# A gated convolution and MLP in one program: the last column of one MLP block computed with the others, and the last output pair loaded inside the loop

## The chip, the cores and the metric

The program runs on one core of a Trainium2 chip. A core has a matrix engine (TensorE, PE in the profile; the loading of its weights is shown as PEld), a vector engine (VectorE, DVE), an activation engine (ScalarE, ACT), a general engine (GpSimd, POOL) and a synchronising engine (SyncE, SP). Each works through its own list of instructions in order and waits on semaphores for the others. SP, ACT and POOL also issue DMA transfers between the large memory (HBM) and the on-chip memory (SBUF); sixteen DMA engines carry them out. Matrix products land in PSUM, eight banks of 128 partitions by 512 floats.

The metric is the time of one execution on the device in microseconds (us); lower is better. The time before is the median of three executions.

## The reference

```
g = sigmoid((x * gate_w).sum(-1))                  # x = A_u, 2048 tokens x 512
a = irfft(rfft(u) * rfft(K)) + u * Dskip           # long convolution; K from A, B, C, dt
b = gelu(B_x @ w1 + b1) @ w2 + b2                  # 512 -> 1792 -> 512
out = g * a + (1 - g) * b
```

All is in float32. The arithmetic of b is called the MLP here and that of a the convolution. The kernel computes b from A_u as its input (the reference passes x = A_u to both).

## The kernel before, in words

The kernel has two parts, one after the other. `front` makes the MLP, the first stage of the convolution's transform of the signal, and the filter's taps (`tk_d`, in HBM). `conv` does the rest of the convolution and the final mix.

**The front.** All of it is written as tasks of a planner (`Plan`). A task has an engine, an estimated duration, the data that it reads and writes, and a due time. `Plan.run` plays the tasks through: whichever engine can start first takes, among its tasks that are ready, the one with the smallest due. The order found in this way is the order in which the instructions are written out; the due times stand in a long string, `DUES`, one number for each task in the order in which the tasks are made. So a task whose due is larger than that of all others is written when its engine has no other task ready.

The MLP takes the 2048 tokens as 8 blocks of 256 and goes over them twice, each time with half of the 14 columns of 128 hidden units: blocks b = 0 to 15 (`NB` = 16), and in each block four steps j = 0 to 3 of 2, 2, 2 and 1 columns. `hidden` makes the hidden values of a step (L985 to L987 on PE, gelu and a rounding on ACT at L1002 and L1005, the low part on DVE at L1012). `output` multiplies them with w2: for each half s of the block's tokens three products for each column (L1028, L1029, L1031) into one of two PSUM accumulators, `acc0` and `acc1`. After a block's last step ACT multiplies the accumulator by 1 - g into a tile `io` (L1053); in the second pass POOL then adds `io` onto the output in HBM with an accumulating DMA (L1066).

Not all of the second pass is done in the front. Of block 15 all w2 products, and of block 14 the last column (j = 3), are put in a list, `late`, which `conv` works off. In block 14 the accumulators are thus closed after j = 2 and go out without their last column.

**The joint.** `conv` has tile pools of its own in the memory that the front's pools leave. In the program of before its first PSUM tiles lie on the front's banks: the signal tiles `p2u` of step 0 on those of `acc0` and `acc1`, those of step 1 on two of the banks of `ph`. The first product tiles `v` of step 0 lie on the bytes of the two `io` tiles. An engine that writes such a tile first waits until the old one has been read.

**The loop of `conv`.** Sixteen steps s. In each, PE makes the second stage of the transform of the signal (`signal`, `p2u`) and of the taps (`taps`, `p2k`, both L1218), DVE multiplies the two (`product`, L1240 to L1245), PE transforms back (`inverse`, `pa`, L1257), ACT copies the result to `sa` (L1269), and SP stores it to `t4_d` in HBM (`turn`, L1271). Beside this POOL loads, in step 6 to 12, one pair of output rows each from HBM (`mix(0)` to `mix(6)`, L1296): the MLP's share to which the convolution's share is to be added. The loads of the last stage's inputs (`quarter`, L1263) are issued by POOL and SP as the groups of eight results are complete, and for the last group by ACT inside `turn(15)`. There `mix(7)`, the load of the last output pair, stands as the last but one of ACT's issues.

**The rest and the last stage.** `rest` works off `late`: three columns before the last `inverse` (`N_REST` = 3), the other thirteen behind the loop, each column three products (L1308 to L1310). The sums of block 14's column (two tiles, `odd`) are multiplied by 1 - g on ACT (L1361) and added on DVE to output pair 6 (L1384); those of block 15 are multiplied and added to output pair 7 in one DVE instruction each (L1379). Then for each of eight pairs of output rows m, PE makes the last product (`pb`, L1373, six PSUM tiles in turn), DVE multiplies it by g and adds it to the loaded pair (L1386), and SP stores the pair (L1392, 512 KB; the last pair in three pieces by SP and ACT, L1390). The two instructions of L1379 stand in DVE's list just before the first of pair 5 and of pair 6.

Of the kernel before, what the change touches and what calls it, by code (L numbers as in the profile page):

```python
# [71 lines left out]
D_SD = -116.26  # L72
D_B2 = 90.72
N_LATE = 2
N_REST = 3
N_LANES = 8
SWITCH = 0.1
# [64 lines left out]
"""  # L142

GROUP = 8
# [205 lines left out]
def gated_mix(  # L350
# [52 lines left out]
    def front(pool, psum, keep, attic, loft, den, pr):  # L403
# [612 lines left out]
        def output(i, t):  # L1016
            b, j = divmod(i, 4)
            fs = cols(i)
            hi, lo, hk, lk = halves(i)

            def products(s, a):
                ss = slice(s * P, (s + 1) * P)
                seeded = b < NSB
                start = j == 0 and not seeded
                for n, f in enumerate(fs):
                    w = f % FH
                    h, l = hi[:, n, ss], lo[:, n, ss]
                    nc.tensor.matmul(a, h, wh[1][w], start=start, stop=False, skip_group_check=seeded)  # L1028
                    nc.tensor.matmul(a, h, wl[1][w], start=False, stop=False, skip_group_check=seeded)  # L1029
                    stop = (j == 2 and n == 1) if b == NB - 2 else j == 3  # L1030
                    nc.tensor.matmul(a, l, wh[1][w], start=False, stop=stop, skip_group_check=seeded)  # L1031
                    start = False

            ws = [(n, f % FH, 1) for f in fs for n in ("wh", "wl")]
            for s in range(2):
                if b == NB - 1 and s >= 2 - N_LATE:
                    for n, f in enumerate(fs):
                        late.append((s, hi[:, n], lo[:, n], wh[1][f % FH], wl[1][f % FH]))
                    continue
                q = (2 * b + s) % N_ACC  # L1040
                n = 3 * len(fs)
                if b == NB - 2 and j == 3:
                    late.append((2 + s, hi[:, 0], lo[:, 0], wh[1][fs[0] % FH], wl[1][fs[0] % FH]))
                else:
                    mm(
                        0.2305 * n, lambda s=s, q=q: products(s, acc[q]), t + LAG + D_OUT * (j == 3),
                        [hk, lk, *ws], [("acc", q)],
                    )
                if j == 3:
                    n = b % NSB * 2 + s  # L1050
                    r = (2 * b + s) % 2
                    act(
                        0.58, lambda n=n, q=q, r=r: nc.scalar.mul(io[r], acc[q], gate[:, 1, n : n + 1]),  # L1053
                        t + D_EV, [("acc", q), ("gate", b % NSB)], [("io", r)],
                    )
                    if b + 1 < NSB:
                        seed(q, t + D_EV)
                    if b < NSB:
                        move(
                            256, lambda n=n, r=r: nc.sync.dma_start(out[n], io[r]), t,  # L1060
                            [("io", r)], [("v", n)],
                        )
                    else:
                        move(
                            512,
                            lambda n=n, r=r: nc.gpsimd.dma_start(out[n], io[r], accum_op=ALU.add),  # L1066
                            t, [("io", r)], [("v", n)], queue="GP",
                        )
# [109 lines left out]
    def conv(pool, ps, late, attic, loft, den, pr):  # L1178
# [86 lines left out]
        def turn(s):  # L1265

            for n in (2 * s, 2 * s + 1):
                sa = sas[n % 6]
                nc.scalar.copy(sa, pas.pop(n))  # L1269
                g, k = divmod(n, GROUP)  # L1270
                nc.sync.dma_start(t4_d[g, :, k].rearrange("e c q d -> (c q) e d"), sa)  # L1271
                if k < GROUP - 1:
                    continue
                if g == 3:
                    for h in (8, 16):
                        quarter(nc.sync, 2, h)
                    for h, n in ((0, 4), (4, 4), (8, 8), (16, 8)):
                        quarter(nc.scalar, g, h, n)
                    quarter(nc.scalar, 2, 24)
                    mix(7, nc.scalar)  # L1280
                    quarter(nc.scalar, g, 24)
                elif g < 2:
                    for h in (0, 8, 24) if g else (0, 8):
                        quarter(nc.gpsimd, g, h)
# [3 lines left out]
        def mix(k, on):  # L1288

            r = 5 + 2 * k if k < 7 else 0  # L1290
            if r < N_ATTIC:
                mos[k] = attic[:, r : r + 2]
            else:
                r -= N_ATTIC
                mos[k] = loft[:, r * D : (r + 2) * D].rearrange("p (s d) -> p s d", s=2)
            on.dma_start(mos[k], out[2 * k : 2 * k + 2].rearrange("s p d -> p s d"))  # L1296
# [32 lines left out]
        for s in range(16):  # L1329

            if s % 2 or s == 0:
                if s < 10:
                    factors((s + 5) // 2)
            for n in range(16 + 4 * s, 20 + 4 * s) if s < 4 else ():
                fetch(n)
            for n in range(2 * s + N_ROOM, min(2 * s + N_ROOM + 2, 32)) if s > 3 else ():
                nc.sync.dma_start(us[n], tu_d[ko[n]])
            product(s)
            if 1 < s + 1 < 16:
                signal(s + 1)  # L1340
            if s + 2 < 16:
                if s and s % 2 == 0:
                    matrices(s // 2 + 1)
                taps(s + 2)
            if s == 15:
                rest(N_REST)
            inverse(s)
            if s == 6:
                quarter(nc.gpsimd, 0, 24)
            if s == 10:  # L1350
                for g in range(2):
                    quarter(nc.gpsimd, g, 16)
            if 6 <= s < 13:
                mix(s - 6, nc.gpsimd)
            if s == 12:
                quarter(nc.gpsimd, 2, 0)
            turn(s)
        rest(16)
        odd = [pool.tile([P, D], F32, tag=f"v{r}", name=f"odd{r}", bufs=2) for r in range(2)]
        for r in range(2):  # L1360
            nc.scalar.mul(odd[r], accs[2 + r], gate[:, 1, 12 + r : 13 + r])  # L1361

        for m in range(8):
            tag = "pa" if m % 3 == 2 else f"pu{m % 3}"
            for i in range(2):
                pb = ps.tile([P, D], F32, tag=f"{tag}{i}", name=f"pb{m}{i}", bufs=1)
                t = 2 * m + i
                parts = [slice(0, D // 2), slice(D // 2, D)] if t == 15 else [slice(0, D)]
                for cs in parts:
                    for b in range(2):  # L1370
                        j = 2 * t + b
                        row = t3[:, j - 8] if j > 7 else den[:, j]
                        nc.tensor.matmul(  # L1373
                            pb[64 * b : 64 * b + 64, cs], g1t[:, min(j, 1)], row[:, cs], start=True, stop=True
                        )
                z = mos[m][:, i]
                if i == 0 and 5 <= m < 5 + N_LATE:
                    r = m - 5
                    nc.vector.scalar_tensor_tensor(  # L1379
                        mos[7][:, r], accs[r], gate[:, 1, 14 + r : 15 + r], mos[7][:, r], ALU.mult, ALU.add  # L1380
                    )
                if m == 1 and i == 0:
                    for r in range(2):
                        nc.vector.tensor_add(mos[6][:, r], mos[6][:, r], odd[r])  # L1384
                for h, cs in enumerate(parts):
                    nc.vector.scalar_tensor_tensor(  # L1386
                        z[:, cs], pb[:, cs], gate[:, 0, t : t + 1], z[:, cs], ALU.mult, ALU.add
                    )
                    if m == 7:
                        (nc.sync, nc.scalar, nc.sync)[i + h].dma_start(out[t][:, cs], z[:, cs])  # L1390
            if m < 7:
                nc.sync.dma_start(out[2 * m : 2 * m + 2].rearrange("s p d -> p s d"), mos[m])  # L1392
# [81 lines left out]
```

## Time and profile before

| what | value |
|---|---|
| time, median of 3 | 506.92 us (506.61 to 507.43) |
| time of the profiled execution | 507.3 us |
| its span, first to last instruction | 505.5 us |
| mean clock granted to TensorE | 0.996 |
| bytes moved by DMA | 107.56 MB |
| output pair loads (L1296) issued by POOL, by ACT | 7, 1 |

The profile shows one execution. Its own time is 1.8 us above its span and 0.4 us above the median. Times within it are counted from its first instruction. A row of the timeline gives start, duration, engine, source line, operation and tiles, and in brackets how long the engine was idle before it and who released it. A "q" behind an engine's name marks an entry of its instruction queue, for instance the issue of a DMA.

### The profile page before, as it was taken

The page shows a single profiled execution, that of the slowest core. Times are in us where ns is not written, and L with a number is a line of the kernel's source. Part 1 is how long each engine was busy: PE and PEld are TensorE (multiplying, and loading weights), DVE is VectorE, ACT ScalarE, POOL GpSimd, SP SyncE. Part 2 cuts the span into 40 slices and gives each one's busy share as a digit, 9 for nine tenths or more (in the row PEclk, how much of TensorE's full clock was granted, in tenths as well). Part 3 has the DMA queues.
Part 4 walks back from the last instruction along what each step waited for, and adds up shares of the span by engine and source line. Part 5 has one row for each costly group of instructions (what it writes and reads, how often), then busy time and mean ns, then how long its engine had stood idle before and what let it go on. Part 6 is the DMA issues. An engine that isn't in the chain of part 4 may idle for free.

```text
span 505.5 us, 12181 instructions
## 1 busy us (share of the span) xinstructions
PE 495.2 (98%) x4802; PEld 379.0 (75%) x4802; DVE 429.2 (85%) x817; ACT 365.0 (72%) x632; POOL 38.3 (8%) x78
## 2 busy tenths in 40 slices
PE   8999999999999999999999999999999999999994
PEld 7898888898989889888988888998989522222551
DVE  4977999999999999999999999999940197877455
ACT  6999997899997789997767998636834465565310
POOL 2000000000000000001010020110100100231000
PEclk9999999999999999999999999999999999999998
DMA  8978686531858622855987244950477999989897
GB/s 286 350 280 278 188 243 213 161 126 43 280 138 246 200 73 72 254 168 116 232 217 241 75 64 128 186 100 3 154 219 169 259 389 389 338 305 391 294 344 299
DMA packets 81569, 107.56 MB, mean 213 GB/s; under 512 B 39284, under 2 KB 43784, under 8 KB 80968
## 3 DMA queue, kind: packets, MB, share of 16 engines
q1 hardware_dynamic: 74792, 82.80, 51.8%
q0 software_dynamic: 6016, 20.70, 15.4%
q10 hardware_dynamic: 704, 3.28, 1.8%
q8 instruction: 38, 0.62, 0.5%
q14 instruction: 19, 0.16, 0.1%
HBM read 61.14 MB, written 45.62 MB: 211 GB/s over the span
## 4 chain that ended last, share of the span: by engine, by line
PE 93%; DMA 2%; SPq 1%; DVE 1%; issue 1%; ACT 0%; POOL 0%; DVEq 0%; POOLq 0%
PE pk L788 12%; PE ph L985 10%; PE acc L1028 10%; PE ph L987 10%; PE ph L986 10%; PE acc L1029 9%; PE acc L1031 9%; PE p2k L1218 5%; PE p2u L1218 5%; PE pa L1257 3%; PE ph L489 3%; PE pb L1373 2%; DMA tk<-tk_d 1%; SPq L830 1%; DMA tk_d<-sk 1%; PE acc L1101 1%
## 5 line engine op out<-in xcount | busy, mean ns | idle before, releaser
L985 PE MATMUL ph<-xh,wh 128*128 128x256 f32 x448 | 127.5, 285 | 0.0
L987 PE MATMUL ph<-xh,wl 128*128 128x256 f32 x448 | 126.8, 283 | 0.0
L986 PE MATMUL ph<-xlo,wh 128*128 128x256 f32 x448 | 126.7, 283 | 0.0
L985 PEld LDWEIGHTS ph<-xh,wh 128*128 128x128 f32 x448 | 85.2, 190 | 6.9 <-issue 4.0
L986 PEld LDWEIGHTS ph<-xlo,wh 128*128 128x128 f32 x448 | 85.1, 190 | 2.1
L987 PEld LDWEIGHTS ph<-xh,wl 128*128 128x128 f32 x448 | 85.2, 190 | 0.0
L1028 PE MATMUL acc<-wh,hh 128*128 128x512 f32 x208 | 84.3, 405 | 0.0
L1029 PE MATMUL acc<-wl,hh 128*128 128x512 f32 x208 | 81.7, 393 | 0.0
L1031 PE MATMUL acc<-wh,hl 128*128 128x512 f32 x208 | 81.4, 391 | 0.0
L1002 ACT ACTIVATE ph<-ph,b1t 128x256 f32<-128x256 f32 x112 | 50.5, 451 | 25.0 <-PE ph L987 23.2
L788 PE MATMUL pk<-y,den 128*32 128x64 f32 x2048 | 61.4, 290 | 0.0
L788 PEld LDWEIGHTS pk<-y,den 128*32 128x32 f32 x2048 | 57.2, 136 | 2.6 <-issue 0.7
L1012 DVE TENSOR_TENSOR hl<-ph,hh 128x512 fp32r<-128x512 f32 (+1 forms) x62 | 38.2, 618 | 18.3 <-ACT hh L1005 10.8
L1028 PEld LDWEIGHTS acc<-wh,hh 128*128 128x128 f32 x208 | 39.1, 188 | 19.4 <-issue 8.8
L750 DVE TENSOR_TENSOR y<-y,ea 128x64 f32<-128x64 f32 (+4 forms) x80 | 45.3, 566 | 0.8 <-POOL y L740 0.3
L1031 PEld LDWEIGHTS acc<-wh,hl 128*128 128x128 f32 x208 | 39.1, 188 | 8.8
L1029 PEld LDWEIGHTS acc<-wl,hh 128*128 128x128 f32 x208 | 39.1, 188 | 6.1
L1226 ACT COPY k<-p2k 128x512 f32<-128x512 f32 x32 | 18.6, 586 | 27.2 <-issue 11.3
L594 DVE TENSOR_TENSOR loft<-den,zz 128x256 f32<-128x256 f32 (+2 forms) x48 | 37.2, 774 | 0.2
L595 DVE TENSOR_TENSOR loft<-den,zz 128x256 f32<-128x256 f32 (+2 forms) x48 | 37.2, 775 | 0.1
L763 DVE TENSOR_TENSOR y<-y,loft 128x2048 f32<-128x2048 f32 x16 | 36.6, 2286 | 0.4 <-ACT loft L713 0.2
L1005 ACT CAST hh<-ph 128x512 fp32r<-128x512 f32 (+1 forms) x62 | 33.0, 533 | 4.3 <-PE acc L1029 2.4
(197 smaller groups left out, 873.3 us busy)
## 6 DMA issues: line engine op xcount, KB each, us to landing
tk_d<-sk SPq DMA_DIRECT2D x32, 256.0 KB, 5.3
t_d<-sa SPq DMA_DIRECT2D x32, 256.0 KB, 5.1
tu_d<-attic SPq DMA_DIRECT2D x40, 128.0 KB, 3.5
attic<-in_xt_dram SPq DMA_DIRECT2D x16, 256.0 KB, 4.3
attic<-in_xs_dram SPq DMA_DIRECT2D x16, 256.0 KB, 5.0
xl_d<-xlo SPq DMA_DIRECT2D x8, 512.0 KB, 5.9
xh_d<-xh SPq DMA_DIRECT2D x8, 512.0 KB, 3.9
out_dram<-io SPq DMA_DIRECT2D x16, 256.0 KB, 3.1
```

What stands on the lines that cost most here:

```text
L594: vec(2 * m, lambda: vv.tensor_mul(t, a, br), due, [ka, *kb], [kt])
L750: nc.vector.tensor_mul(both(n, 64 - 3 * n, n), both(0, 64 - n, n), an)
L788: nc.tensor.matmul(pks[q][32 * j : 32 * j + 32, :, gg], x[:, r, :, ch], y[:, r, :, ch], start=(r == 0), stop=(r == 1), skip_group_check=True,)
L985: nc.tensor.matmul(p, h, xh[xk][:, d], start=(d == 0), stop=False)
L986: nc.tensor.matmul(p, h, xlo[xk][:, d], start=False, stop=False)
L987: nc.tensor.matmul(p, lo, xh[xk][:, d], start=False, stop=(d == 3))
L1002: nc.scalar.activation(phs[q][:, n], phs[q][:, n], AF.Gelu_apprx_tanh, bias=b1t[:, f : f + 1])
L1012: nc.vector.tensor_sub(lo, phs[q][:, 0:nf], hi.bitcast(F32))
L1028: nc.tensor.matmul(a, h, wh[1][w], start=start, stop=False, skip_group_check=seeded)
L1029: nc.tensor.matmul(a, h, wl[1][w], start=False, stop=False, skip_group_check=seeded)
L1031: nc.tensor.matmul(a, l, wh[1][w], start=False, stop=stop, skip_group_check=seeded)
L1218: nc.tensor.matmul(out[64 * i : 64 * i + 64], w, x, start=True, stop=True)
```

## The change

There are three edits that belong together.

1. Block 14's last column is no longer put off. `ODD = ()` names the halves whose column would be; being empty, it makes `output` add six products (three for each half of the tokens) as two tasks of the front, and move the accumulators' closing to them. Both tasks get the due 10000, which is larger than every other. The multiplication at L1053 and the accumulating DMA at L1066 of block 14 now come behind these tasks. In `conv` the six products of `rest`, the two ACT multiplications (L1361) and the two DVE additions (L1384) fall away.
2. `mix(7)` moves from ACT's issues in `turn(15)` to POOL's in step 13 of the loop. In POOL's list it then stands behind `quarter(2, 0)` of step 12.
3. The two DVE instructions that add block 15's sums to output pair 7 move from their places before pairs 5 and 6 to a place before the whole last stage.

```diff
+ODD = ()
...
-1773 415 2550 11 2497 14 320 242 499 507 544 671 244 133 477 228 163 91 19 193 589 536 459 592 210 132 229
...
+1773 415 10000 2550 11 10000 2497 14 320 242 499 507 544 671 244 133 477 228 163 91 19 193 589 536 459 592
...
-                    stop = (j == 2 and n == 1) if b == NB - 2 else j == 3
+                    stop = (j == 2 and n == 1) if b == NB - 2 and s in ODD else j == 3
...
-                if b == NB - 2 and j == 3:
+                if b == NB - 2 and j == 3 and s in ODD:
                     late.append((2 + s, hi[:, 0], lo[:, 0], wh[1][fs[0] % FH], wl[1][fs[0] % FH]))
...
                     quarter(nc.scalar, 2, 24)
-                    mix(7, nc.scalar)
                     quarter(nc.scalar, g, 24)
...
-            if 6 <= s < 13:
+            if 6 <= s < 14:
                 mix(s - 6, nc.gpsimd)
             if s == 12:
                 quarter(nc.gpsimd, 2, 0)
...
-        odd = [pool.tile([P, D], F32, tag=f"v{r}", name=f"odd{r}", bufs=2) for r in range(2)]
-        for r in range(2):
+        odd = {r: pool.tile([P, D], F32, tag=f"v{r}", name=f"odd{r}", bufs=2) for r in ODD}
+        for r in ODD:
             nc.scalar.mul(odd[r], accs[2 + r], gate[:, 1, 12 + r : 13 + r])

+        for r in range(N_LATE):
+            nc.vector.scalar_tensor_tensor(
+                mos[7][:, r], accs[r], gate[:, 1, 14 + r : 15 + r], mos[7][:, r], ALU.mult, ALU.add
+            )
...
-                if i == 0 and 5 <= m < 5 + N_LATE:
-                    r = m - 5
-                    nc.vector.scalar_tensor_tensor(
-                        mos[7][:, r], accs[r], gate[:, 1, 14 + r : 15 + r], mos[7][:, r], ALU.mult, ALU.add
-                    )
                 if m == 1 and i == 0:
-                    for r in range(2):
+                    for r in ODD:
                         nc.vector.tensor_add(mos[6][:, r], mos[6][:, r], odd[r])
```

6 rows, old and new, of the table DUES are left out of this document.

## The prediction

> **What bounds the kernel now.** I read the page first, then the chain of work that ended last, then the timelines of the two places that the change touches, then the transfers there. First the shares of the chain by engine, and two pieces of the chain in order of time (start, us, what):
>
> ```profile
> PE 93%; DMA 2%; SPq 1%; DVE 1%; issue 1%; ACT 0%; POOL 0%; DVEq 0%; POOLq 0%
> ...
> 396.56 5.76 DMA tk<-tk_d
> ...
> 402.36 2.49 PE p2k L1218 x8
> ```
>
> PE carries 93% of the chain. It leaves PE at two places. At the joint between front and conv it runs over the store and the reload of the taps: the first tap tile is issued at 396.56, lands at 402.32, and PE starts on it at 402.36. The other place is the end, behind PE's last products. So work moved from the tail into the front is paid in full on PE unless the joint has room, and what it saves is only what the tail's own limit gives back.
>
> The tail, by the stretch (PE, PEld, DVE, ACT, POOL busy, clock, DMA share, GB/s):
>
> ```profile
> 473.00:478.00 5.00, 5.00 (x26) 3.22 (x25) 1.60 (x3) 1.93 (x4) 0.00 (x0) 1.00 0.64 232
> 478.00:483.00 5.00, 5.00 (x24) 4.14 (x23) 0.00 (x0) 0.00 (x0) 0.00 (x0) 1.00 0.98 333
> 483.00:494.00 11.00, 11.00 (x52) 4.42 (x52) 7.59 (x12) 1.26 (x2) 0.00 (x0) 1.00 0.98 354
> 494.00:501.00 7.00, 4.93 (x28) 1.72 (x24) 5.97 (x10) 0.00 (x0) 0.00 (x0) 1.00 1.02 391
> ```
>
> From 478 to 501 the DMA engines are full (0.98 to 1.02). Between 473 and 478 they are not (0.64, so 1.8 us of 5 idle). DVE looks as full behind 486, and the chain of waits ends in DVE; it does not show a queue in which a transfer stands after its issue. These rows do: SP's first stores, the landing of the first of them (issued at 487.74), that of the last pair's pieces, and the two queues (packets, MB, share) in 483 to 490, then SP's in 494 to 500.
>
> ```profile
> 487.74 4.63 SPq L1392 DMA_DIRECT2D out_dram<-attic  x3
> ...
> DMA to landing us min/median/max: 7.8/7.8/7.8
> ...
> DMA to landing us min/median/max: 4.5/4.6/4.6
> ...
> q10 hardware_dynamic: 435, 2.46, 97.5%
> q1 hardware_dynamic: 3, 0.00, 0.0%
> ...
> q1 hardware_dynamic: 1207, 2.32, 100.9%
> ```
>
> The store of 487.74 (SP's q1) moved nothing before 490: ACT's loads (q10) held the engines. Stores then drain at 2.32 MB in 6 us at full share, 0.387 MB/us, or 1.36 us for a pair of 512 KB (0.524 MB). Eight pairs need 10.8 us, and the last pieces still take 4.5 us, where a 256 KB store with free engines takes 2.4 (quoted below). So I read the tail as **bound by bytes**: it ends when the loads are in and eight pairs have drained, not when DVE is done.
>
> **The change, part by part.**
>
> *Six products into the front.* The timelines of PE, its weight loads and ACT at the joint:
>
> ```profile
> 391.96 0.39 PE L1028 MATMUL acc<-wh,hh 128*128 128x512 f32 x1
> ...
> 394.71 0.28 PE L985 MATMUL ph<-xh,wh 128*128 128x256 f32 x1
> ...
> 397.46 0.28 PE L987 MATMUL ph<-xh,wl 128*128 128x256 f32 x1
> 397.67 3.65 PE L1218 MATMUL p2u<-den,pr 128*64 128x512 f32 x16
> ...
> 399.16 0.43 PEld L1218 LDWEIGHTS p2u<-den,pr 128*64 128x64 f32 x4 [0.43 <-DVE hl L1012]
> ...
> 402.91 0.19 PEld L1218 LDWEIGHTS p2k<-tk,pr 128*64 128x64 f32 x3 [0.36 <-DMA tk<-tk_d]
> ...
> 394.91 0.69 ACT L1053 ACTIVATE io<-acc,gate 128x512 f32<-128x512 f32 x1 [0.60 <-PE acc L1031]
> ...
> 398.27 0.37 ACT L1005 CAST hh<-ph 128x256 fp32r<-128x256 f32 x1
> ```
>
> Twelve such products ran from 391.96 to 394.71, 0.229 each; six cost 1.37. A due above all others puts them where PE has nothing else ready, and PE has no gap there: behind the last hidden product (397.46 + 0.12 = 397.58), ending at 398.95. The three of the first half end at 397.58 + 0.69 + 0.16 (a product's 0.39 outlasts its 0.23 pace) = 398.43. ACT is busy until 398.27 + 0.37 = 398.64, and its two multiplications of 0.69 now come behind that, to 399.35 and 399.95. Step 0's signal tiles lie on the banks that they read, so this is a new wait: PE stands before `p2u` until 399.4, with everything behind it in its list, instead of starting at 397.67. The second tile is free in time. The old wait of 0.43 at 399.16 for DVE is over by then. Sixteen products at 0.215 end at 399.4 + 3.44 = 402.84, against 402.36, when the first tap tile was used. But the second tap tile held PE until 402.91 in any case, and the first sum needs both. So 1.73 us of delay meets as much slack: between -0.07 (both tiles needed; PE itself is busy until 402.84, so earlier tap tiles bring no more) and 0.48 (the first half counts); I take **0.05**, by the second row. Without this cover it would cost 1.73. What is late next is the DMA again, not PE.
>
> *The accumulating DMAs of block 14.* POOL's second issue, the landing of all fourteen of L1066, and what DVE and PE do next:
>
> ```profile
> 395.89 0.86 POOL L1066 DMA_DIRECT2D out_dram<-io  x1 [0.43 <-ACT io L1053]
> ...
> DMA to landing us min/median/max: 4.0/5.0/7.6
> ...
> 404.64 0.69 DVE L1240 TENSOR_TENSOR v<-p2u,k 128x512 f32<-128x512 f32 x1 [5.54 <-ACT k L1226]
> 405.50 0.69 DVE L1241 TENSOR_TENSOR v<-p2u,k 128x512 f32<-128x512 f32 x1 [0.17 <-ACT k L1226]
> ...
> 407.90 0.68 DVE L1245 TENSOR_TENSOR v<-v,z 128x512 f32<-128x512 f32 x1
> ...
> 408.85 0.21 PEld L1257 LDWEIGHTS pa<-v,pr 64*64 64x64 f32 x8 [0.81 <-DVE v L1245]
> ```
>
> They follow ACT by 0.3 (395.60 to 395.89), so at 399.65 and, POOL needing 0.86 for each, 400.5. With the fourteen issues' landing of 4.0 to 7.6, median 5.0, `io` is free at 404.65 and 405.5, just when DVE first writes `v` there (404.64, 405.50). A late landing holds all six DVE products behind it; PE waits for them only beyond 0.27 (408.58 to 408.85). Bounds 0 and 408.1 - 405.5 - 0.27 = 2.3; I take **0.1**, near the median. Nothing else stands behind them in POOL's queue until the loop's sixth step.
>
> *The load of pair 7.* Its issue on ACT, POOL's last entry, SP's last stores of `t_d`, the landing of the last two of these, and ACT's first load:
>
> ```profile
> 484.13 0.79 ACTq L1296 DMA_DIRECT2D attic<-out_dram  x1
> ...
> 471.36 0.55 POOL L1263 DMA_DIRECT2D den<-t_d  x1 [7.89 <-DMA t_d<-sa]
> ...
> 471.07 6.79 SPq L1271 DMA_DIRECT2D t_d<-sa  x5
> ...
> DMA to landing us min/median/max: 2.4/2.4/2.4
> ...
> 479.96 1.15 ACTq L1263 DMA_DIRECT2D den<-t_d  x2
> ```
>
> Its 0.524 MB leave the full stretch: 1.36 at the drain's pace, 1.48 at the 354 GB/s of its own stretch; I take **-1.45**. Only one of ACT's issues, the last `quarter`, was behind it. On POOL it stands behind the `quarter` of 471.36, thus at 471.9, and nothing after it. Its bytes then run in 473 to 478, where 1.8 us is free, but beside the last five stores of `t_d` (from 471.07), the last two of which now land in 2.4 us and release ACT's loads at 479.96. What doesn't fit pushes these: 0 if the gaps take all, 1.36 if the stores wait for the whole of it. I take **+0.25**, near the low end since the gaps are wider than the load.
>
> *The end of DVE's list.* PE's first products of the last stage, the landing of ACT's first loads, four rows of DVE, and the landing of all pair loads (L1296):
>
> ```profile
> 484.97 3.65 PE L1373 MATMUL pb<-den,g1t 128*64 128x512 f32 x16
> ...
> DMA to landing us min/median/max: 4.6/4.6/4.6
> ...
> 487.62 1.28 DVE L1384 TENSOR_TENSOR loft<-loft,odd 128x512 f32<-128x512 f32 x2
> 488.83 2.72 DVE L1386 SCALAR_TENSOR_TENSOR attic<-pb,gate,attic 128x512 f32<-128x512 f32 x4
> ...
> 494.49 0.74 DVE L1379 SCALAR_TENSOR_TENSOR attic<-acc,gate,attic 128x512 f32<-128x512 f32 x1
> 495.15 1.40 DVE L1386 SCALAR_TENSOR_TENSOR loft<-pb,gate,loft 128x512 f32<-128x512 f32 x2
> ...
> DMA to landing us min/median/max: 7.1/8.9/12.6
> ```
>
> PE's `rest` ends 1.37 sooner, at 483.6, but the last group's first rows, issued at 479.96, land after 4.6: the last stage can start at 484.6, 0.4 sooner than 484.97. DVE loses two additions (487.62 to 488.83, 1.21) and has the two instructions of L1379 (494.49 to 495.15, 0.66 each) done before the first product; their wait for pair 7 (471.9 + 12.6 = 484.5 at the longest) holds nobody. That is 2.53 + 0.4 sooner for the stores. The two ACT multiplications that fall away were on no path. As the stores queue at the engines, I count **0**; it would be 2.9 if that queue were not there.
>
> Sum: 0.05 + 0.1 - 1.45 + 0.25 = **-1.05**, all in the profiled execution: 507.3 becomes 506.25. That execution is 0.4 above the median, which I carry: 506.92 - 1.05 = **505.9 us**.
>
> **The rivals.**
>
> *DVE ends the tail.* For it: the chain ends in DVE, and DVE is full from 486. Against it: the stores' 7.8 and 4.5 us. Then -2.9 + 0.15 = 504.2.
>
> *The moved load meets the last stores.* For it: in the loop, with the engines full, `t_d` stores take far longer than 2.4 (landing of all of L1271 from 440 on):
>
> ```profile
> DMA to landing us min/median/max: 2.4/5.3/10.9
> ```
>
> If the two queues share evenly, the last two stores' 0.524 MB take twice 1.36: +1.36 in place of +0.25, 507.0, no change. The Trainium skill (DMA: Bandwidth & Descriptors, "Queues, rings and completion order") says that each engine goes round the queues with work, packet by packet, which speaks for this; the trace's q1, empty beside a full q10 at 487.74 to 490, disagrees. If the last store takes the loop's median of 5.3, the loads start 2.9 late: -1.45 + 2.9 + 0.15 = +1.6, **508.5, slower**. It decides at 1.3 us: beyond it the change loses.
>
> *The joint pays.* An `io` landing of 6.2 to 7.6, or the full 0.48 before the taps, gives +0.5 to +2.3: 506.3 to 508.1, mostly no change.
>
> *The products come elsewhere than last.* In an earlier gap of the planner's PE they delay `p2u` to 399.04 instead of 399.4; the time is the same, and it needs no case of its own.
>
> **How the numbers follow.** Forecast 505.3 to 506.4: 0.49. DVE ends it: 0.12. Even sharing: 0.13. Stores late: 0.14. Joint: 0.12. A measurement tells 0.2% (1.0 us) from no change. The forecast lies on that line, with a little more of it beyond: 0.31 faster, 0.18 same. The joint splits 0.08 same, 0.04 slower. So faster 0.31 + 0.12 = 0.43, same 0.18 + 0.13 + 0.08 = 0.39, slower 0.14 + 0.04 = 0.18. The range goes from the DVE case (504.2, with 0.2 off) to 507.4, leaving out the late stores and the worst joint, 0.18. The forecast's own range is 505.3 to 506.4.
>
> **What would show it.** Right: six L1028 to L1031 products behind the last L987; `p2u` about 1.7 later after ACT's L1053, and the first `p2k` at most 0.5 later; POOL's eighth L1296 near 472; ACT's last `quarter` one issue sooner; DVE finished some 3 us sooner, with the stores' landing longer than 4.5 at the end. Wrong: last-pair landings near 2.4 (DVE was the bound), or ACT's first `quarter` over 1 us later against the loop's end (the stores were pushed), or DVE's first L1240 waiting on an L1066 DMA.

## The result, and the profile after

| | before | after |
|---|---|---|
| time, median of 5 | 506.92 us (506.18 to 508.78) | 511.14 us (509.39 to 512.50) |
| ratio, 95% interval | 1 | 1.0061 [1.0040, 1.0083] |
| profiled execution, its span | 507.3, 505.5 us | 509.79, 507.9 us |

The change makes the kernel **slower by 0.6%**, and the interval leaves out both no change and the forecast of 505.9. The ratio is not the quotient of the two medians; these lie 4.2 us, or 0.8%, apart, at the upper end of the interval. The profiled executions differ by 2.4 us in their span. I take that difference apart first; of the line numbers after, those from the front and the loop are one higher.

The joint, by PE's timeline of the kernel after (start, us, instruction, idle time before it and releaser):

```profile
398.32 0.28 PE L988 MATMUL ph<-xh,wl 128*128 128x256 f32 x1
398.44 0.39 PE L1029 MATMUL acc<-wh,hh 128*128 128x512 f32 x1
...
399.60 0.39 PE L1032 MATMUL acc<-wh,hl 128*128 128x512 f32 x1
400.15 3.65 PE L1219 MATMUL p2u<-den,pr 128*64 128x512 f32 x16 [0.16 <-ACT io L1054]
403.64 3.68 PE L1219 MATMUL p2k<-tk,pr 128*64 128x512 f32 x16
...
411.69 1.68 PE L1258 MATMUL pa<-v,pr 64*64 64x512 f32 x8 [2.05 <-DVE v L1245]
```

The last hidden product starts at 398.32, 0.86 later than before (397.46). This much was late since the first loads of the program, which the change does not touch; an execution starts with such a scatter. The six products follow the last hidden one. `p2u` waits for ACT's `io` and is 2.48 later than before, thus 1.62 beside the scatter. The taps are not late: `p2k` starts at 403.64, where the one that mattered before started at 402.91 (0.73 later, no more than the scatter). So far all went as forecast. But the first inverse, `pa`, waits 2.05 for DVE. DVE's timeline there, then POOL's and SP's issues, then, from the view of one line's instructions, the landing of POOL's two DMAs (the first, their mean and the second):

```profile
407.15 0.69 DVE L1241 TENSOR_TENSOR v<-p2u,k 128x512 f32<-128x512 f32 x1 [7.18 <-ACT f L402]
409.15 0.69 DVE L1242 TENSOR_TENSOR v<-p2u,k 128x512 f32<-128x512 f32 x1 [1.31 <-DMA out_dram<-io]
...
411.55 0.69 DVE L1246 TENSOR_TENSOR v<-v,z 128x512 f32<-128x512 f32 x1
```

```profile
400.39 1.75 POOL L1067 DMA_DIRECT2D out_dram<-io  x2 [28.83 <-ACT io L1054]
```

```profile
397.11 2.41 SPq L1198 DMA_DIRECT2D tk<-tk_d  x4
399.56 0.43 SPq L1190 DMA_DIRECT2D cc<-in_c_dram  x1
400.03 1.86 SPq L1198 DMA_DIRECT2D tk<-tk_d  x4
```

```profile
DMA to landing us min/median/max: 6.6/7.3/8.0
```

The two issues start at 400.39 and 401.01. DVE's second instruction names the DMA that reads `io1` as what it waited for; that DMA landed at 401.01 + 8.0 = 409.0. The first instruction is put down to ACT, but it begins at 407.15, and the DMA that reads `io0` landed at 400.39 + 6.6 = 407.0: where the time fits so closely, I take it to be that DMA. `e1` and `e6` below bear this out: without that wait DVE begins at 404.40, before ACT has made `f`. This is the sign that the prediction gave for being wrong.

What the joint lost stays. The last copy that ACT makes in the loop (here of before and of after), ACT's first load of the tail, and the DMA engines in the stretches of the tail of after (last two columns: share, GB/s):

```profile
476.08 1.07 ACT L1269 COPY sa<-pa 128x512 f32<-128x512 f32 x2 [2.23 <-issue]
```

```profile
479.49 1.08 ACT L1270 COPY sa<-pa 128x512 f32<-128x512 f32 x2 [2.21 <-issue]
484.04 1.65 ACTq L1264 DMA_DIRECT2D den<-t_d  x2
```

```profile
473.00:478.00 5.00, 5.00 (x29) 2.31 (x25) 4.11 (x7) 2.15 (x4) 1.28 (x2) 1.00 0.57 159
478.00:483.00 5.00, 5.00 (x26) 3.26 (x25) 0.64 (x2) 1.08 (x2) 0.00 (x0) 1.00 1.12 413
483.00:494.00 11.00, 8.96 (x41) 4.90 (x41) 3.97 (x7) 0.00 (x0) 0.00 (x0) 1.00 0.92 316
494.00:501.00 7.00, 7.00 (x35) 2.80 (x33) 6.14 (x9) 0.00 (x0) 0.00 (x0) 1.00 0.97 369
```

From these rows come the three parts by which I compare all runs below. **The loop's end** is 479.49 - 476.08 = 3.41 late: 0.86 from the start and 2.55 from the joint. **The push**, from that copy to ACT's first load, is 4.55 against 3.88 (479.96 - 476.08), 0.67 more. **Behind it**, from that load to the end of the span, are 23.9 against 25.6, 1.65 less. The sum, 3.41 + 0.67 - 1.65, is the 2.4 us of the spans. The stretch of 473 to 478 has the gap of before (0.57, before 0.64), and the moved load, issued behind that gap, runs in the next stretch (1.12): the loop lies 3.4 later against these borders.

Where the gain behind that load arises, the end of the last stage shows. First before: PE's last products, DVE's last instructions, and the landing of the last pieces stored; then the same of after:

```profile
488.45 10.47 PE L1373 MATMUL pb<-t,g1t 128*64 128x512 f32 x52
498.44 1.53 DVE L1386 SCALAR_TENSOR_TENSOR attic<-pb,gate,attic 128x512 f32<-128x512 f32 x3
...
DMA to landing us min/median/max: 4.5/4.6/4.6
```

```profile
492.80 10.53 PE L1377 MATMUL pb<-t,g1t 128*64 128x512 f32 x52 [0.69 <-DMA t<-t_d]
502.50 1.74 DVE L1385 SCALAR_TENSOR_TENSOR attic<-pb,gate,attic 128x512 f32<-128x512 f32 x3
...
DMA to landing us min/median/max: 2.7/2.8/3.0
```

DVE ends at 499.97 before and at 504.24 after, 20.0 and 20.2 us behind ACT's first load: it is not done sooner. It ends 1.05 us behind PE's last product before and 0.9 after, so in both kernels it keeps pace with PE. PE's 68 products of this stage take 13.95 us before (from 484.97) and 13.97 in `e8` below, where they also run without a pause; after they take 14.9, with the wait of 0.69 in them. The gain lies behind DVE: from its end to the end of the span are 5.5 us before and 3.7 after, since the last pieces land 1.8 us faster.

### The profile page after: what moved, and what is told of

It is laid out like the page before. It is cut to its first block, busy times and chain, and to the rows that moved or that the text cites. A ratio compares the mean times of both kernels' runs of the same rounds, so it can differ in the third digit from the quotient of the medians.

```text
span 507.9 us, 12176 instructions
## 1 busy us (share of the span) xinstructions
PE 496.4 (98%) x4802; PEld 380.4 (75%) x4802; DVE 429.1 (84%) x815; ACT 363.7 (72%) x630; POOL 39.1 (8%) x79
## 4 chain that ended last, share of the span: by engine, by line
PE 84%; ACT 9%; DMA 3%; issue 2%; DVE 1%; ACTq 0%; POOL 0%; DVEq 0%; SPq 0%; POOLq 0%
PE pk L789 12%; PE acc L1029 9%; PE ph L986 9%; PE ph L988 9%; PE ph L987 9%; PE acc L1030 8%; PE acc L1032 8%; PE p2u L1219 6%; PE p2k L1219 4%; PE pa L1258 3%; PE ph L490 3%; PE pb L1377 2%; DMA t<-tk_d 1%; DMA t<-t_d 1%; ACT ph L1003 1%
```

## The experiments

Theory A: the accumulating DMAs of block 14 now land so late that DVE must wait to write the first product tiles, which lie on the bytes that they read. The rival: the products and multiplications themselves, or the traffic in whatever order, cost the time. A second question is why the moved load brings so little. All ratios are to the kernel before, timed on the same chip, with the 95% interval (each experiment 12 runs, `e4` 6, a seventh of 1175 us being left out, against 29 to 35 of before, whose medians were 507.55 to 507.86). The last three columns are the differences to before of the three parts above, in us, worked out in the same way from one profiled execution of each.

| kernel | ratio | loop's end | push | behind |
|---|---|---|---|---|
| changed kernel | 1.0061 [1.0040, 1.0083] | +3.41 | +0.67 | -1.65 |
| e1: after, `io` elsewhere | 0.9991 [0.9973, 1.0008] | +1.39 | +1.33 | -2.73 |
| e2: before, `io` elsewhere | 0.9995 [0.9978, 1.0012] | +1.28 | +0.12 | +0.34 |
| e6: after, no DMAs of block 14 | 0.9979 [0.9964, 0.9994] | -0.26 | +0.72 | -1.44 |
| e5: after, products early | 0.9987 [0.9968, 1.0006] | +0.38 | +1.57 | -2.20 |
| e4: column alone, late | 1.0083 [1.0055, 1.0112] | +4.38 | +0.01 | -0.50 |
| e10: column alone, early | 0.9986 [0.9966, 1.0006] | +1.28 | +0.01 | +0.24 |
| e3: load alone | 0.9997 [0.9977, 1.0016] | -0.31 | +1.79 | -1.98 |
| e7: load left out | 0.9977 [0.9963, 0.9991] | +0.61 | +0.02 | -1.63 |
| e9: load alone, issued first | 0.9979 [0.9966, 0.9993] | +1.35 | +0.02 | -1.69 |
| e8: products early, load first | 0.9968 [0.9953, 0.9983] | -0.25 | +0.03 | -1.81 |
| e11: after, load first | 1.0053 [1.0034, 1.0073] | +3.35 | +0.06 | -2.01 |

The loop's end of one execution holds its scatter at the start (between -0.4 and +1.0 here), so it is read with the rows that name the wait, and the verdict is the ratio. The landing of the taps scatters too: `e7`, whose front and joint are those of before, is 0.96 late beside its scatter at the start (-0.35), because its first tap tile comes later. The three parts are thus good to about 1 us at the joint.

**e1: the place of `io`.** One line of the front moves up, so that the two `io` tiles take bytes that `conv` later gives to `sa0` and `sa1`, which ACT first writes behind the first inverse.

```diff
+        io = tiles(2, [P, D], "io")
         sk = pool.tile([P, 64, 2, 4, 8], F32, name="sk")
...
-        io = tiles(2, [P, D], "io")
```

> The changed kernel with one line moved: the two io tiles are allotted first in the front's pool, so that they lie under sa0 and sa1 of the loop (first written some 6 us after the first product) and no longer under the product tiles v. Theory A (the loop's first product waits for block 14's accumulating DMAs, because v lies on io; price at the joint 2.6 us): DVE's first L1240/L1241 no longer wait on a DMA, the first inverse comes at most 0.5 later than before the change against the end of the hidden products, and the time is that of before less the tail's 1.0: 505.5 to 506.5, clearly below the changed kernel's 511.1. Theory B (the price is PE's: 1.37 of products and the wait for ACT on the accumulators' banks): nothing changes, 509.5 to 512.

Measured: 0.9991, the whole slowdown is gone. The 507.13 us miss the 505.5 to 506.5 expected, though: the push of 1.33 takes half of what the tail gains. DVE's and PE's rows of this kernel:

```profile
404.40 0.69 DVE L1241 TENSOR_TENSOR v<-p2u,k 128x512 f32<-128x512 f32 x1 [5.39 <-ACT k L1227]
```

```profile
399.19 3.65 PE L1219 MATMUL p2u<-den,pr 128*64 128x512 f32 x16 [0.16 <-ACT io L1054]
402.68 3.68 PE L1219 MATMUL p2k<-tk,pr 128*64 128x512 f32 x16
407.57 1.46 PE L1219 MATMUL p2k<-tk,cc 128*64 128x512 f32 x3 [1.21 <-ACT k L1227]
```

The products stand where they stood, `p2u` is as late (399.19 with no scatter at the start), the DMAs are issued at 399.4 and 400.1 and take 7.1 and 9.3 us, and DVE begins at 404.40, before either has landed. So neither the products nor the late `p2u` cost it: the wait does. Some 1.4 us stay at the joint, where 0.5 at most were expected. ACT's copies of the factors wait for their load, and behind them PE waits for one more tap tile; ACT's row and PE's weight loads name the two:

```profile
406.07 0.41 ACT L401 ACTIVATE f<-cc 64x256 f32<-64x256 f32 x1 [0.85 <-DMA cc<-in_c_dram]
...
408.38 0.13 PEld L1219 LDWEIGHTS p2k<-tk,cc 128*64 128x64 f32 x1 [0.63 <-DMA tk<-tk_d]
```

These loads of SP share the engines with the same two DMAs; without the DMAs (`e6`) `pa` starts at 408.62 and not at 410.25. The wait was the larger of two effects, and takes the smaller in when it is there.

**e2: the control**, the same line moved in the kernel before.

> The kernel before with the same line moved: the control for the new places of all the front's tiles. Both theories: the time of before within 0.3% (505.5 to 508.5), since block 14's accumulating DMAs were done there before the first product.

Measured 0.9995. The move by itself does nothing that can be told.

**e6: without the two DMAs.** Block 14's two additions onto the output are left out, so its share of the second pass is missing there; products and multiplications stay.

```diff
-                            lambda n=n, r=r: nc.gpsimd.dma_start(out[n], io[r], accum_op=ALU.add),
+                            lambda n=n, r=r: None if b == NB - 2 else nc.gpsimd.dma_start(out[n], io[r], accum_op=ALU.add),
```

> The changed kernel without the two accumulating DMAs of block 14, so two of the output's sixteen tiles lack their second share; products, multiplications and places stay. Theory A (the wait for these DMAs is what the change lost): the inverse products at the joint start where they do in the kernel before or up to 0.5 us earlier, and the whole comes out 0.8 to 2 us below the kernel before (ratio 0.996 to 0.9985). Theory B (the products and multiplications ahead of p2u cost it): the joint stays 1.5 to 2.5 late, ratio 1.003 to 1.006.

PE's timeline at the joint:

```profile
399.20 3.65 PE L1219 MATMUL p2u<-den,pr 128*64 128x512 f32 x16 [0.16 <-ACT io L1054]
402.68 3.68 PE L1219 MATMUL p2k<-tk,pr 128*64 128x512 f32 x16
...
408.62 1.09 PE L1258 MATMUL pa<-v,pr 64*64 64x512 f32 x8
```

Measured 0.9979. `p2u` is 1.5 late and `pa` 0.24 early (408.86 before): the delay of PE by the products is covered in full, as the prediction had it. All that the joint lost hangs on the two DMAs.

**e5: the products early.** The two tasks get the lowest due in place of the highest.

```diff
-1773 415 10000 2550 11 10000 2497 14
+1773 415 0 2550 11 0 2497 14
```

> The changed kernel with the two added product tasks given the lowest due in place of the highest, so that they follow their block's other products and block 14's two accumulating DMAs are issued before SP's tap loads instead of among them. Theory A (the slowdown is DVE's first product tile waiting until those DMAs, issued at 400.4 and 401.0, land): they are issued near 396.5 and 397.5, land near 402 and 404, before DVE first writes the tiles at 404.6; the joint costs 0 to 0.5 and the whole comes out 0.2 to 1.0 us below the kernel before (ratio 0.998 to 1.000). Theory B (the six products in the front, or the traffic at the joint whatever its order, cost the 2 to 3 us): as the changed kernel, ratio 1.004 to 1.008.

POOL's two issues, their landing, and DVE's first product:

```profile
395.26 0.86 POOL L1067 DMA_DIRECT2D out_dram<-io  x1 [24.50 <-DMA tk_d<-sk]
397.31 0.86 POOL L1067 DMA_DIRECT2D out_dram<-io  x1 [1.19 <-ACT io L1054]
```

```profile
DMA to landing us min/median/max: 5.9/6.1/6.2
```

```profile
405.04 0.69 DVE L1241 TENSOR_TENSOR v<-p2u,k 128x512 f32<-128x512 f32 x1 [4.51 <-ACT k L1227]
```

Measured 0.9987. They land at 401.2 and 403.5, before DVE starts at 405.04, and nobody waits for them. The same traffic in another order costs nothing that can be told, so it is not the traffic as such. The prediction had said that the place of the products makes no difference to the time. For the DMAs behind them it makes 0.7% (0.9987 against 1.0061).

**e4 and e10: the column alone**, with the load of pair 7 and its two DVE instructions back at their old places; in `e4` the products come last, in `e10` early.

```diff
                     quarter(nc.scalar, 2, 24)
+                    mix(7, nc.scalar)
                     quarter(nc.scalar, g, 24)
...
-            if 6 <= s < 14:
+            if 6 <= s < 13:
```

> Block 14's column in the front, but the load of pair 7 on ACT in the last step and the two instructions before pairs 5 and 6, as before. Theory A: the joint's 2.0 to 3.0 in full and nothing of the tail's gain from the load; DVE's two additions are gone, which saves 0 if the tail is bound by bytes (time 509 to 510.5) and 1.2 if DVE ends it (507.8 to 509). Theory B: the same sum, so this run tells only what the load is worth.

> The column's move alone, with its products early; the load of pair 7 stays in the tail as in the kernel before. Theory C: no change, ratio 0.9990 to 1.0005, last stores at the spacing of 1.3 as before. Theory D: 0.998 to 0.999, the end 0.5 to 1 us sooner. If the wait for the accumulating DMAs is not the cause of what the column alone lost (ratio 1.0083), it stays near 1.007.

Measured 1.0083 and 0.9986. The column is the whole loss, and only in its late place. The 511.44 us of `e4` lie above the 509 to 510.5 expected; the last section has a reason that its trace shows. Whether the column brings a little when early can't be told: the interval of `e10` has 1 in it.

**e3 and e7: the load alone, and no load.** `e3` handles the column as before and has the load at its new place. `e7` leaves that load out, so the output's last pair lacks the MLP's first share.

```diff
-ODD = ()
+ODD = (0, 1)
...
-1773 415 10000 2550 11 10000 2497 14
+1773 415 2550 11 2497 14
```

```diff
-            on.dma_start(mos[k], out[2 * k : 2 * k + 2].rearrange("s p d -> p s d"))
+            if k < 7:
+                on.dma_start(mos[k], out[2 * k : 2 * k + 2].rearrange("s p d -> p s d"))
```

> The load of pair 7 in the loop and the two instructions of L1379 ahead of the last stage, but block 14's column put off as before (ODD = (0, 1), no due 10000). Theory A: no io wait, the tail's gain alone: 0.8 to 1.4 below before, 505.5 to 506.1. Theory B says nothing else here. If the moved load pushes the last stores (the rival of the prediction), the time is 507 or more.

> The kernel that has the load's move alone (block 14's last column handled as before), now without the load of pair 7 at all, so the output's last two tiles lack their first share. Theory P (in the move's new place the load's 0.52 MB pushes the last stores of t_d by 1.3 to 1.8 us and so gives back what it saves behind them): without it the last stores land as in the kernel before, 2.4 us after their issue, ACT's first loads start where they did, and the end comes 1.2 to 2.0 us earlier than before (ratio 0.996 to 0.9975). Theory Q (the bytes of that load bound nothing, the tail hangs on DVE or on PE): within 0.3 us of the kernel before, ratio 0.9995.

POOL's entries, the landing of the last two stores of `t_d`, ACT's first load and the stretches in `e3` (in these the last two columns are DMA share and GB/s), with the first stretch of before behind them:

```profile
470.07 0.55 POOL L1264 DMA_DIRECT2D den<-t_d  x1 [6.90 <-DMA t_d<-sa]
470.62 0.73 POOL L1296 DMA_DIRECT2D attic<-out_dram  x1
```

```profile
DMA to landing us min/median/max: 4.2/4.2/4.2
```

```profile
481.44 1.47 ACTq L1264 DMA_DIRECT2D den<-t_d  x2
```

```profile
470.00:473.00 3.00, 3.00 (x19) 1.00 (x16) 2.38 (x4) 1.14 (x4) 1.28 (x2) 1.00 0.61 127
473.00:478.00 5.00, 5.00 (x26) 3.21 (x25) 1.31 (x3) 1.64 (x4) 0.00 (x0) 1.00 0.97 362
478.00:483.00 5.00, 5.00 (x24) 4.13 (x22) 0.75 (x1) 0.00 (x0) 0.00 (x0) 1.00 0.88 315
```

```profile
470.00:473.00 3.00, 3.00 (x18) 0.85 (x15) 2.11 (x5) 1.14 (x3) 0.55 (x1) 1.00 0.92 273
```

Measured: 0.9997 with the load moved, 0.9977 without it. Its bytes are worth 1.63 us behind ACT's first load (`e7`), near the forecast's 1.45. In its new place it fills 473 to 478 (0.97, before 0.64), and the last two stores, issued in that stretch, land after 4.2 us instead of 2.4. ACT's loads wait for them, 1.8 us longer than before. The engines idle in 470 to 473 (0.61, before 0.92) and in 478 to 483 (0.88, before 0.98) instead. The gap has moved; it has not gone.

Nor was the gap room for a load. In the kernel before, SP's queue moved 0.03 MB from 473 to 475, although three of its stores, issued at 471.1, 473.4 and 474.0, had not landed (they took 5.5, 3.8 and 3.9); POOL's queue moved 0.32 MB there, of the quarter issued at 471.36. In `e3` this standstill is longer: from 470 to 473 SP's queue moved 0.00 MB, with stores issued at 470.2 and 470.8 that took 6.6 and 7.9, while POOL's moved 0.36. The idle share is thus time in which stores stood behind their issue. Why they stand while POOL's quarter begins, no run shows.

**e8, e9 and e11: the load ahead of the quarter.** In POOL's list the load stood behind `quarter(2, 0)`, which waits for stores until 470. Here it goes first: `e8` with the products early, `e9` with the column as before, `e11` with the products last.

```diff
-            if s == 12:
+            if s == 13:
                 quarter(nc.gpsimd, 2, 0)
```

> The kernel with the products early, and on POOL the load of pair 7 now ahead of the quarter that is issued in step 12 and waits there for stores; the quarter follows it. Theory P (the load costs what it pushes the last stores of t_d by): it is issued up to 3 us earlier, and its bytes use the stretch of 470 to 473 where the engines had 0.4 to 0.6 of their time busy; the last stores are pushed by under 1 us and the end comes 0.5 to 1.0 us before the kernel with the products early alone. Theory R (the engines are full until 470, so that earlier bytes push earlier stores as much): no difference to it, within 0.3 us.

> The load's move alone, with POOL's load of pair 7 ahead of the quarter that waits for stores; block 14's last column is handled as in the kernel before. Theory C (the column's move, once its DMAs go early, is worth nothing, since PE and DVE have time to spare behind the loop): as the kernel with both, ratio 0.996 to 0.998, the end 1.4 to 1.8 us before the kernel before. Theory D (the six products fewer in the tail and the two additions that DVE loses are worth 0.5 to 1 us of their own): 0.998 to 0.9995.

> The changed kernel as it is, products last, with POOL's load of pair 7 ahead of the quarter that waits for stores. The joint keeps its 2 to 3 us, the last stores of t_d land 2.4 us after their issue in place of 3.1: the two effects add up, and it comes out 0.4 to 1.0 us below the changed kernel, ratio 1.003 to 1.006. If the two aren't independent (the late joint gives the engines time, so that the load pushes nothing there), it equals the changed kernel, 1.006.

The same rows of `e8`:

```profile
467.10 0.72 POOL L1296 DMA_DIRECT2D attic<-out_dram  x1 [3.88 <-PE p2u L1219]
470.57 0.56 POOL L1264 DMA_DIRECT2D den<-t_d  x1 [2.75 <-DMA t_d<-sa]
```

```profile
DMA to landing us min/median/max: 2.4/2.4/2.5
```

```profile
479.74 1.15 ACTq L1264 DMA_DIRECT2D den<-t_d  x2
```

```profile
470.00:473.00 3.00, 3.00 (x19) 1.00 (x16) 2.34 (x4) 1.14 (x3) 0.56 (x1) 1.00 1.12 323
473.00:478.00 5.00, 5.00 (x26) 3.23 (x25) 1.34 (x3) 1.67 (x4) 0.00 (x0) 1.00 0.65 250
478.00:483.00 5.00, 5.00 (x23) 4.14 (x23) 0.75 (x1) 0.00 (x0) 0.00 (x0) 1.00 0.99 355
```

Issued 3.5 us sooner, the load has landed at 472.9 (5.8 after its issue), and the engines are full in 470 to 473 (1.12, in `e3` 0.61, before, without the load, 0.92); the last stores land after 2.4 again, the push is 0.03, and the gain behind is kept. `e8` measures **0.9968 [0.9953, 0.9983]**, 0.3% faster than the kernel before and faster than the changed one. `e9` (0.9979) shows that most of this is the load's; the intervals of `e8` and `e9` overlap, so what the column adds is open. `e11` (1.0053) still pays the joint. That the load's place in POOL's list matters rests on the rows (a push of 0.02 to 0.06 in all three): by the ratios alone `e8` can't be told from `e5`, `e9` from `e3`, or `e11` from the changed kernel, as their intervals overlap.

## Why the prediction was wrong

- **The accumulating DMAs of block 14: this step failed.** It was put at 0.1, with 2.3 as the far bound; the joint cost 2.55, and all of it is this step, since `p2k` was not late. The prediction put the second issue at 400.5 and took the median landing, 5.0, of all fourteen issues. The issue was not late: 401.01, or 400.15 without the scatter. The landing was: 8.0, past the longest of the fourteen. The median mixes issues that had little beside them and issues in a crowd: four of the fourteen, with no traffic of SP's in the next 5 us, landed after 4.0 to 4.2, and the other ten, beside SP's transfers, after 4.2 to 7.6. The nearest rows, the same two DMAs in the kernel before, took 5.1 and 6.2. What should have been seen: before, these DMAs were issued ahead of SP's tap loads, and the taps bore the wait (the first tap tile, issued at 396.56, took 5.76); after, six of SP's nine issues shown above start before POOL's first, and the engines are full (a share of 1.06 from 401 to 409). The order of the two was exchanged. After, PE found both first tap tiles in time at 403.64, issued from 397.11 on, and the DMAs now stand behind. "The joint pays" had the right mechanism, and its price of 0.5 to 2.3 held most of it; its chance of 0.12 was too low, since the 6.2 of the nearest row already reaches it.
- **The products' delay and its cover: right.** `p2u` 1.62 late beside the scatter (forecast 1.73), `p2k` not at all; `e6` shows the joint without the DMAs 0.2 early.
- **The load off the tail: right in size, its signs only in part.** -1.45 forecast, -1.65 in the changed kernel, -1.63 with the load left out. The gain does lie in the stores' queue behind DVE, 5.5 us before and 3.7 after. But the prediction expected landings over 4.5 us to stay at the end, with DVE done some 3 us sooner; the last pieces landed after 2.8, and DVE was not done sooner. Once the load is gone, the drain of eight pairs no longer sets the end: PE's products of the stage do, with a short store behind them.
- **What its bytes push: too small.** 0.25 forecast. It was 0.7 in the changed kernel and in `e6`, and 1.3 to 1.8 in `e1`, `e3` and `e5`, which have the same order in POOL's list; one execution of each doesn't tell what decides. In `e3` it eats the gain almost whole. The rival in which the load and the stores share the engines evenly put it at 1.36. The Trainium skill's rule that it named (DMA: Bandwidth & Descriptors, "Queues, rings and completion order"), each engine going round the queues that have work, agrees with a part of `e3`: from 473 to 476 POOL's queue moved 0.65 MB and SP's 0.37, side by side. It does not fit the standstill of SP's queue from 470 to 473 (0.00 MB, with two stores issued). The step's reason, gaps wider than the load, took that standstill for room: the stores came with the gap, just ahead of the loads that wait for them.
- **The end of DVE's list at nothing: the number fits, the reason does not.** The two DVE instructions and the additions are gone from its end, and DVE still ends 0.9 us behind PE's last product, 1.05 before. The work that it lost had run beside PE's products. The reason given was the stores' queue; the rows show PE's pace. No run changed DVE's list alone.

So the forecast's sum had two terms too low, by 2.4 and 0.4, and the gain in the tail too low by 0.2; 0.86 of the profiled difference is the start's scatter. The ratio's 0.6% is 3.1 us (2.0 to 4.2 by its interval). That is 1.5 more than the parts without the scatter (2.55 + 0.67 - 1.65 = 1.6) give; about 1 us of it may be the scatter of the taps at the joint, and the last section has another candidate.

## What to carry to other kernels

When a producer is moved later, price its last consumer, not its first: here a DMA's read of a buffer that the next stage's first output overwrites, and take its landing from rows in the same crowd of transfers, not from a median over the kernel. Moving a transfer out of a full stretch paid here only where no store with a waiting load behind it shared the new place; the same load, 3.5 us earlier in its queue, kept its gain in the profile. A low DMA share is not yet room: look whether transfers that have been issued stand still in it. A planner that can't see what lies behind its own part can place last the work that nobody in that part waits for, and here the buffers' next owners paid for it.

## What the runs showed of the hardware

In `e4` PE's pause at the joint was followed by a drop of the granted clock (column before the last two: 1.00, then 0.50):

```profile
408.80:411.00 2.20, 0.00 (x0) 0.00 (x0) 2.20 (x5) 0.53 (x2) 0.00 (x0) 1.00 1.06 407
411.00:412.50 1.50, 1.49 (x8) 0.39 (x8) 1.50 (x3) 0.54 (x2) 0.00 (x0) 0.95 1.06 393
412.50:415.50 3.00, 3.00 (x11) 0.80 (x10) 3.00 (x6) 1.07 (x2) 0.00 (x0) 0.50 1.07 376
```

PE did nothing from 408.8 to 411.0, ran on at the full clock, and from 412.4 to 415.8 at half of it; the loop's end is 4.38 late in this execution, against 2.55 without the scatter in the changed kernel, whose profiled execution paused 2.05 us and kept 1.00. In none of the other twelve profiles does the clock fall while PE still has work. The Trainium skill (TensorE: Matmul & The Clock Gate, "What's actually happening") puts the fall to half clock after an idle window of about 3.4 us that runs freely; here a pause of 2.2 us was enough, once. A pause near this length that costs 1.8 us more (4.38 - 2.55) in some executions than in others would explain why the changed kernel's runs reach from 509.39 to 512.50 and why its median lies above what its profile adds up to. That is argued, not shown: only one execution of it was traced. The mean clock of a run does not settle it, because it also falls when PE is done: before it was 0.996, with half clock only in its last 4.4 us, behind PE's last product.
